# Reordering the issue of splits, control operations and a row list in the second stage of an attention and two-layer expert kernel

## The chip, the cores and the metric

One core of a Trainium2 chip. The metric is device time in microseconds (us) of the whole program. TensorE (PE) multiplies and has a queue of weight loads beside it (PEld); DVE, ACT and POOL are the vector, scalar and general engines; SP issues most of the transfers (DMA).

## The reference

Three stages follow each other on 4,608 tokens of 512 features (8 batches of 576 positions, 8 heads of 64). What is computed in the part that the change touches is the last one:

```python
attn_out = _attn_ref(q, k, v, phi)                     # attention through 32 memory slots a head
x = attn_out.transpose(0, 2, 1, 3).reshape(B * S, H * D)
x = elu(x @ w_in) @ w_out                              # 512 -> 2048 -> 512, every token
logits = x @ w_gate                                    # 8 experts
expert_idx = argmax(logits, axis=1)
gate_w = softmax(logits)[arange(N), expert_idx]
for e in range(8):
    xe = x[expert_idx == e]
    out[expert_idx == e] = gate_w[...] * (maximum(xe @ w1[e], 0) @ w2[e])   # 512 -> 1024 -> 512
```

All data is float32. Each product is made of three matmuls on pairs of rounded parts (high x high, low weights x high, high weights x low), so each operand is first "split" into a high part (a cast on ACT) and a low part (a subtraction on DVE).

## The kernel before

**First stage.** Attention and the first expert-like layer run over 16 halves of 288 tokens. At the end of each half the rows of x, times the gate, are written to a table in HBM (y_turn, y_gate, y_times on DVE, y_store on SP), and a list of the rows of each expert is scattered to another (y_scatter).

**Second stage (phase2, lines 946 to 1379).** The tokens of each expert are cut into tiles of 288. Two tiles of the expert of the first token (tiles -2 and -1, e = -2 in the code) are known early and begin while the last half is still being routed; then come 14 slots (slot(0) to slot(13), tiles 0 to 13) of full tiles, and then steps that are decided at run time (some, many). For a tile, mm1(j, f) is the first product for a block f of 128 of the 1,024 hidden features (12 matmuls of 128x128 on 288 tokens into one of two PSUM banks, ps_h), with its ReLU split into hh (ACT, L1088) and hl (DVE, L1089); mm2(j, f) adds the second product of that block (12 matmuls, ps_acc). They alternate: mm1 runs two blocks ahead of mm2, and mm1(j+1, 0) and mm1(j+1, 1) run in the last two steps (f = 6, 7) of slot j. A bank of ps_h is free again when hh and hl of the product of two before have read it.

**The weights.** load(j, i) (SP, L940) brings w1 (i = 0) or w2 (i = 1) of slot j's expert to raw[0] or raw[1], 2,048 KB each, under a condition that is read from the table ctl: where the expert is that of the slot before, it moves nothing. w1_split and w2_split (L1067 to L1074) then make the parts, 16 of them in a slot, two in each step f, for the next slot: w1 in f = 0 to 3, w2 in f = 4 to 7. In the two early tiles w2's eight splits for weights set 0 are issued between the products by hand.

**The tokens.** gather(j) (POOL, three indirect DMAs) brings the rows of a tile to the buffer xr; x_store writes them to HBM in xd and x_load reads them back to xg in another order; x_turn (DVE, four transposes) and x_split(j, c) (four chunks c: a cast on ACT, L749, and a subtraction on DVE, L750) make the operands xh and xl. Results go the other way: evac (DVE) to ot, o_store to od in HBM, o_load back to the same xr, and scatter (POOL) to the output. There is one xr, one xg, one xd and one od, so these steps of neighbouring tiles form one chain.

**The lists.** slots() computes on DVE which rows each slot has and issues an indirect DMA for the lists (its); control() computes ctl (which load to do) and the loop ends, 18 small DVE operations. columns() turns the lists by four small transposes on TensorE (L1042, L1045), with DVE operations before and behind (L1039, L1046 to L1049); gather(0) needs what it makes.

The order of the work on every engine is the order in which the program issues it (it is written out by hand under a manual schedule), and each engine takes its own instructions in that order; waits come from what an instruction reads and writes.

Of the kernel before, what the change touches and what calls it, by code (L numbers as in the profile page):

```python
# [57 lines left out]
def attn_moe_moe2_kernel(  # L58
# [112 lines left out]
    with ExitStack() as order:  # L171
        order.enter_context(tc.manual_schedule())
        setup()
        with ExitStack() as p1, ExitStack() as late_pool:
# [744 lines left out]
            mm2(b, g, f)  # L919
            y_evac(b, g)  # L920
            phase2(nc, tc, locals())


# [22 lines left out]
def phase2(nc, tc, a):  # L946
# [9 lines left out]
    early, early_w, pool, xp, x_gather, x_store, x_load, o_store, o_load, x_turn, x_split, early_gather = (  # L956
        a[n] for n in (
            "early", "early_w", "pool", "xp", "x_gather", "x_store", "x_load", "o_store", "o_load", "x_turn",
            "x_split", "early_gather",
        )  # L960
    )
# [58 lines left out]
    def control():  # L1020
        pick(sj, ind, st)
        pick(ej, ind, erow)
        V.tensor_scalar(out=later, in0=pcol, scalar1=0.0, scalar2=None, op0=ALU.is_gt)
        V.scalar_tensor_tensor(out=ctl[:, 0:1], in0=sj, scalar=pcol, in1=later, op0=ALU.is_equal, op1=ALU.mult)
        V.tensor_copy(out=ctl[:, 1:2], in_=ej)
        pick(sj, ind, ne)
        V.tensor_tensor(out=row, in0=row, in1=jm, op=ALU.add)
        V.scalar_tensor_tensor(out=row, in0=ej, scalar=-float(NR0), in1=row, op0=ALU.mult, op1=ALU.add)
        V.scalar_tensor_tensor(out=sj, in0=row, scalar=-float(T), in1=sj, op0=ALU.mult, op1=ALU.add)
        V.tensor_scalar(out=ctl[:, 2:3], in0=sj, scalar1=float(FEW), scalar2=1.0, op0=ALU.is_le, op1=ALU.add)  # L1030
        V.tensor_copy(out=ends[:, 0:1], in_=tot)
        V.tensor_copy(out=ends[:, 1:2], in_=few)
        V.scalar_tensor_tensor(
            out=ends[:, 2:3], in0=tot, scalar=float(NMIN + 1), in1=few, op0=ALU.is_gt, op1=ALU.max
        )

    def columns():
        itf = xp["r"][0:NS].rearrange("p n d -> p (n d)")[:, 0:T]
        V.tensor_copy(out=itf, in_=its)  # L1039
        ps = ps_tile(ps_m, "m")  # L1040
        for n in range(NG):
            nc.tensor.transpose(  # L1042
                ps[0:PR, NS * n:NS * n + NS], itf.rearrange("j (p n) -> j n p", n=NG)[:, n], ident[0:NS, 0:NS],
            )
        nc.tensor.transpose(ps[0:FEW, NS * NG:NS * NG + NS], itf[:, 0:FEW], ident[0:NS, 0:NS])  # L1045
        V.tensor_copy(out=idf, in_=ps[0:FEW, NS * NG:NS * NG + NS])  # L1046
        ps = ps[0:PR, 0:NG * NS]
        V.tensor_scalar(out=idx, in0=ps, scalar1=float(NT - 1), scalar2=None, op0=ALU.min)
        V.tensor_copy(out=idw, in_=ps)  # L1049

    def of(t, j):
        return lambda n: t[:, NS * n + j:NS * n + j + 1]

    def gather(j):
        for n in range(NG):
            x_gather(n, of(idx, j)(n), rows)
# [4 lines left out]
    def w1_at(p, y, c, f):  # L1061
        return wt0[:, y, 2 * c + f // HN, p, P * (f % HN):P * (f % HN) + P]

    def w1_split(p, n):
        h, l = (wt0[:, y, 2 * (n % NC) + n // NC, p] for y in range(2))
        x = raw[0][:, 512 * (2 * (n % NC) + n // NC):][:, 0:512]
        nc.scalar.copy(out=h, in_=x)  # L1067
        V.tensor_tensor(out=l, in0=x, in1=h.bitcast(F32), op=ALU.subtract)

    def w2_split(p, f, eng=V):  # L1070
        h, l = (w2t[p][:, y, f].rearrange("p (c x i) -> p c x i", c=NC, i=32) for y in range(2))
        x = raw[1][:, DM * f:DM * f + DM].rearrange("p (x c i) -> p c x i", c=NC, i=32)
        nc.scalar.copy(out=h, in_=x)
        eng.tensor_tensor(out=l, in0=x, in1=h.bitcast(F32), op=ALU.subtract)  # L1074
# [3 lines left out]
    def mm1(j, f):  # L1078
        p = max(j, 0) % 2
        xh, xl = xp[j]  # L1080
        ps = ps_tile(ps_h, "h")[:, 0:T]
        n = 0
        for y, x in ((0, xh), (1, xh), (0, xl)):
            for c in range(NC):
                nc.tensor.matmul(ps, w1_at(p, y, c, f), x[:, c], start=(n == 0), stop=(n == 3 * NC - 1))  # L1085
                n += 1
        h, l = (pool.tile([P, T], F32R, tag=f"g{x}", name=f"h{x}", bufs=3) for x in "hl")
        nc.scalar.activation(out=h, in_=ps, func=AF.Relu)  # L1088
        V.scalar_tensor_tensor(out=l, in0=ps, scalar=0.0, in1=h.bitcast(F32), op0=ALU.max, op1=ALU.subtract)  # L1089
        hq[j, f] = h, l  # L1090

    def mm2(j, f):
        p = max(j, 0) % 2
        h, l = hq.pop((j, f))
        for c in range(NC):
            if f == 0:
                acc[c] = ps_tile(ps_acc, f"acc{c}")[:, 0:T]
        for n, (y, x) in enumerate(((0, h), (1, h), (0, l))):
            for c in range(NC):
                nc.tensor.matmul(  # L1100
                    acc[c], w2t[p][:, y, f, P * c:P * c + P], x,
                    start=(f + n == 0), stop=(f == NF2 - 1 and n == 2),
                )

    def evac(j):
        ot = xp["o"]
        for c in range(NC):
            V.transpose(out=ot[:, :, c], in_=acc[c].rearrange("p (k t) -> p k t", t=32))

    def scatter(at, alone=False):  # L1110
        o_load()
        for n in range(NG):
            d = nc.gpsimd.indirect_dma_start(  # L1113
                out=out, out_offset=IndirectOffsetOnAxis(ap=at(n), axis=0), in_=xp["r"][:, n], in_offset=None,
                bounds_check=NT - 1, oob_is_err=False,
            )
            if not alone:
                rows_out(d)

    def load(j, i):  # L1120
        c, = (nc.values_load(ctl[j:j + 1, 0:1], engines=[SP], min_val=0, max_val=1),)
        ev = nc.values_load(ctl[j:j + 1, 1:2], engines=[SP], min_val=0, max_val=E - 1)
        load_raw(nc, raw[i], (w1, w2)[i], ev, c)

    def rows_out(d):
        tc.declare_no_dep(d.ins, group="rows", reason="a token's row is its own")
        tc.add_to_no_dep_group("rows", d.ins)

    def splits(j, some):
        for n in some:  # L1130
            w1_split(j % 2, n) if n < NF2 else w2_split(j % 2, n - NF2)

    def x_splits(j, some=range(NC)):
        for c in some:
            x_split(j, c)

    def slot(j):
        follow = j + 1 < NMIN
        if j > 0:
            o_store(ONE)  # L1140
        if j < NMIN - 1:
            gather(j + 2)
        if 0 < j < NMIN - 1:
            x_store()
        if j > 0:
            scatter(of(idw, j - 1))
        for f in range(NF2):
            if f + 2 < NF2:
                mm1(j, f + 2)
            elif follow:  # L1150
                mm1(j + 1, f + 2 - NF2)
            mm2(j, f)
            if f == NF2 - 1:
                evac(j)
                if not follow:
                    o_store(ONE)
                    scatter(of(idw, j))
            splits(j + 1, range(2 * f, 2 * f + 2))
            if f == 3:
                x_turn(j + 1)  # L1160
            if f in (4, 5):
                x_splits(j + 1, range(2 * f - 8, 2 * f - 6))
            if follow and f == HN - 1:
                load(j + 2, 0)
                if j == 0:
                    x_store()
            if follow and f == NF2 - 2:
                x_load()
            if follow and f == NF2 - 1:
                load(j + 2, 1)  # L1170
# [71 lines left out]
    e = -NE  # L1242
# [18 lines left out]
        y_turn(b, g, c)  # L1261
    for i in range(2):
        y_gate(b, g, i)
    y_times(b, g, 0, NB)
    y_store(b, g)
    mm1(e, 4)
    mm2(e, 2)
    w2_split(0, 4)
    w2_split(0, 5)
    control()  # L1270
    load(1, 0)
    mm1(e, 5)
    mm2(e, 3)
    for c in range(NC):
        x_split(-1, c)
    w2_split(0, 6)
    w2_split(0, 7)
    load(1, 1)
    mm1(e, 6)
    mm2(e, 4)  # L1280
    mm1(e, 7)
    mm2(e, 5)
    mm1(e + 1, 0)
    mm2(e, 6)
    mm1(e + 1, 1)
    mm2(e, 7)
    evac(e)
    mm1(e + 1, 2)
    mm2(e + 1, 0)
    columns()  # L1290
    gather(0)
    x_store()
    x_load()
    o_store(ONE)
    scatter(early_of(e))
    mm1(e + 1, 3)
# [29 lines left out]
    for j in range(NMIN - 1):  # L1326
        slot(j)
# [18 lines left out]

    first = kind(NMIN)
    slot(NMIN - 1)
    with tc.If(end > NMIN):
        either(NMIN, first)  # L1350
# [61 lines left out]
```

## Time and profile before

| | |
|---|---|
| time of three runs | 1264.07, 1264.52, 1267.41 us; median 1264.52 |
| profiled execution | 1260.01 us, its span 1258.3 us |
| busy share: PE, PEld, DVE, ACT, POOL | 96%, 88%, 63%, 53%, 36% |
| granted TensorE clock, mean | 0.985 of full speed |
| DMA | 178.41 MB, mean 142 GB/s |
| second stage | from 811.16 us (first product of tile -2) |
| slots 1 to 12 | 897.83 to 1211.06 us |

The span runs from the first to the last instruction; the time is that of the device around it. Times in the rows are counted from the span's start. The shares are averages over stages with different limits. A row of the timeline gives the start, the duration of the merged instructions, engine, line, operation with the tiles it writes and reads, the shapes and the number merged; in brackets is the idle time of the engine just before, and what ended it. "slot 2, step 6" is slot(2), f = 6.

### The profile page before, as it was taken

Reading aid. Unit: us, or ns where it says so; the run is one execution under the profiler, and the core shown is the slowest. Engines: PE = TensorE matmul, PEld = TensorE weight load, DVE = VectorE, ACT = ScalarE, POOL = GpSimd, SP = SyncE. Lnnn points to the kernel's source line nnn. Section 1 sums busy time; section 2 is a strip of 40 time slices with the busy share of each in tenths; the row PEclk is TensorE's granted clock in tenths of the full one; section 3 lists DMA queues with packets and bytes.
Section 4 is the critical chain, followed back from the end, with each engine's and each line's share of the span. In section 5 each row is a group of like instructions: output and inputs, shape, how many; then the busy total and the mean of one; then the engine's idle time right before and its main releaser. Section 6 shows DMA issues by size and latency. Waiting matters only on the chain.

```text
span 1258.3 us, 26270 instructions
## 1 busy us (share of the span) xinstructions
PE 1202.6 (96%) x10035; PEld 1110.3 (88%) x10035; DVE 789.9 (63%) x1816; ACT 664.6 (53%) x1526; POOL 450.3 (36%) x489
## 2 busy tenths in 40 slices
PE   5598899999999999999999999999999999999997
PEld 3387789899899898898899899999999999999994
DVE  6989666556556556556556535663676767767672
ACT  4687455555655555555555555522454444544542
POOL 3544244444434534434534544322212311321202
PEclk9599999999999999999999999999999999999999
DMA  9776677446356436435442271215578778566763
GB/s 260 221 220 197 175 116 153 124 96 105 106 96 105 126 75 107 136 63 112 131 64 58 69 209 33 64 21 150 153 187 255 214 215 247 151 143 191 216 212 98
DMA packets 113786, 178.41 MB, mean 142 GB/s; under 512 B 10745, under 2 KB 79609, under 8 KB 110064
## 3 DMA queue, kind: packets, MB, share of 16 engines
q1 hardware_dynamic: 105632, 157.09, 49.3%
q0 software_dynamic: 8016, 19.52, 5.5%
q8 instruction: 82, 1.34, 0.5%
q14 instruction: 56, 0.46, 0.2%
HBM read 171.62 MB, written 42.76 MB: 170 GB/s over the span
## 4 chain that ended last, share of the span: by engine, by line
PE 74%; DVE 8%; DMA 7%; issue 4%; ACT 3%; POOL 1%; SPq 1%; POOLq 0%; DVEq 0%; ACTq 0%
PE ps_acc L553 27%; PE ps_h L521 15%; PE ps_h L1085 13%; PE ps_acc L1100 11%; DMA kv<-in_v_dram 4%; PE ps_M L483 2%; PE ps_kv L381 2%; PE ps_s L425 1%; DMA out_dram<-xr,idw 1%; PE ps_l L575 1%; DVE conv_h L290 1%; DVE conv_h L293 1%; PE ps_a L373 1%; DMA xd<-xr 1%; PE ps_l L585 1%
## 5 line engine op out<-in xcount | busy, mean ns | idle before, releaser
L539 POOL TENSOR_TENSOR gl<-e,gh 128x288 fp32r<-128x288 f32 x234 | 193.4, 826 | 379.3 <-ACT gh L538 312.2
L521 PE MATMUL ps_h<-ath,wt 128*128 128x288 f32 x1024 | 260.0, 311 | 8.3 <-DVE e L531 5.6
L531 DVE SCALAR_TENSOR_TENSOR e<-e,ps_h 128x288 f32<-128x288 f32 x247 | 110.2, 447 | 205.1 <-ACT e L529 190.9
L521 PEld LDWEIGHTS ps_h<-ath,wt 128*128 128x128 f32 x1024 | 180.3, 190 | 53.1 <-issue 30.8
L538 ACT CAST gh<-e 128x288 fp32r<-128x288 f32 x247 | 106.8, 432 | 182.3 <-DVE e L531 179.2
L553 PE MATMUL ps_acc<-gh,wt 128*128 128x288 f32 x1024 | 179.2, 297 | 1.5 <-ACT gh L538 1.5
L553 PE MATMUL ps_acc<-gh,wl 128*128 128x288 f32 x1024 | 178.2, 296 | 0.0
L553 PE MATMUL ps_acc<-gl,wt 128*128 128x288 f32 x1024 | 177.4, 295 | 0.3 <-DVE gl L539 0.3
L1088 ACT ACTIVATE hh<-ps_h 128x288 fp32r<-128x288 f32 x128 | 52.7, 412 | 221.7 <-PE ps_h L1085 186.3
L1085 PE MATMUL ps_h<-xh,wt 128*128 128x288 f32 x1024 | 164.6, 300 | 1.9 <-ACT xh L749 0.7
L553 PEld LDWEIGHTS ps_acc<-gh,wt 128*128 128x128 f32 x1024 | 151.0, 190 | 3.5 <-ACT gh L538 2.4
L521 PE MATMUL ps_h<-atl,wt 128*128 128x288 f32 x512 | 151.9, 297 | 0.5 <-POOL atl L471 0.5
L1085 PEld LDWEIGHTS ps_h<-xh,wt 128*128 128x128 f32 x1024 | 144.3, 188 | 8.6 <-ACT xh L749 5.2
L553 PEld LDWEIGHTS ps_acc<-gl,wt 128*128 128x128 f32 x1024 | 150.6, 188 | 0.5 <-DVE gl L539 0.5
L553 PEld LDWEIGHTS ps_acc<-gh,wl 128*128 128x128 f32 x1024 | 150.6, 190 | 0.0
L1089 DVE SCALAR_TENSOR_TENSOR hl<-ps_h,hh 128x288 fp32r<-128x288 f32 x128 | 58.2, 455 | 120.2 <-ACT hh L1088 105.0
L528 ACT ACTIVATE e<-ps_h 128x288 f32<-128x288 f32 x256 | 104.8, 409 | 44.9 <-PE ps_h L521 43.6
L1113 POOL DMA_INDIRECT out_dram<-xr,idw x42 | 42.4, 1010 | 239.9 <-DMA xr<-od 215.1
L529 ACT ACTIVATE e<-e 128x288 f32<-128x288 f32 x256 | 113.9, 445 | 8.1
L521 PEld LDWEIGHTS ps_h<-atl,wt 128*128 128x128 f32 x512 | 98.2, 192 | 0.7 <-POOL atl L471 0.7
L1085 PE MATMUL ps_h<-xl,wt 128*128 128x288 f32 x512 | 89.5, 296 | 1.0 <-DVE xl L750 1.0
L1100 PE MATMUL ps_acc<-hh,wl 128*128 128x288 f32 x576 | 88.5, 296 | 0.0
(217 smaller groups left out, 1920.0 us busy)
## 6 DMA issues: line engine op xcount, KB each, us to landing
raw<-in_moe_w_dram SPq DMA_DIRECT2D x30, 2048.0 KB
win<-win_s SPq DMA_DIRECT2D x28, 1024.0 KB
xd<-xr SPq DMA_DIRECT2D x17, 576.0 KB
xg<-xd SPq DMA_DIRECT2D x68, 144.0 KB
kv<-in_k_dram SPq DMA_DIRECT2D x16, 576.0 KB
kv<-in_v_dram SPq DMA_DIRECT2D x16, 576.0 KB
table<-yr SPq DMA_DIRECT2D x64, 144.0 KB
od<-ot SPq DMA_DIRECT2D x64, 144.0 KB
```

The costliest lines, as they stand in the source:

```text
L521: nc.tensor.matmul(ps, x[:, u, fo:fo + P], y[:, u], start=(n == 0), stop=(n == 3 * NQ - 1))
L528: nc.scalar.activation(out=e, in_=ps, func=AF.Relu, scale=-1.0)
L529: nc.scalar.activation(out=e, in_=e, func=AF.Exp, scale=-1.0)
L531: nc.vector.scalar_tensor_tensor(out=y, in0=e, scalar=-1.0, in1=ps, op0=ALU.add, op1=ALU.max)
L538: nc.scalar.copy(out=gh, in_=e)
L539: eng.tensor_tensor(out=gl, in0=e, in1=gh.bitcast(F32), op=ALU.subtract)
L553: nc.tensor.matmul(acc[c], x[:, f, P * c:P * c + P], y, start=(first and n == 0), stop=(final and n == 2),)
L1085: nc.tensor.matmul(ps, w1_at(p, y, c, f), x[:, c], start=(n == 0), stop=(n == 3 * NC - 1))
L1088: nc.scalar.activation(out=h, in_=ps, func=AF.Relu)
L1089: V.scalar_tensor_tensor(out=l, in0=ps, scalar=0.0, in1=h.bitcast(F32), op0=ALU.max, op1=ALU.subtract)
L1100: nc.tensor.matmul(acc[c], w2t[p][:, y, f, P * c:P * c + P], x, start=(f + n == 0), stop=(f == NF2 - 1 and n == 2),)
L1113: d = nc.gpsimd.indirect_dma_start(out=out, out_offset=IndirectOffsetOnAxis(ap=at(n), axis=0), in_=xp["r"][:, n], in_offset=None, bounds_c ...
```

## The change

Issue order alone is changed. In each slot the x_splits of steps 4 and 5 are issued ahead of the splits of those steps. In the hand-written order of the two early tiles y_times and y_store move behind mm1(e, 4); the splits 5, 6 and 7 of w2 and the control operations move behind later products, splits 6 and 7 behind load(1, 1); the splits of tile -1's tokens move behind mm1(e, 6); and columns(), gather(0), x_store and x_load move from behind mm2(e+1, 0) to behind mm1(e+1, 1).

```diff
--- before.py
+++ after.py
@@ -1155,11 +1155,11 @@
                 if not follow:
                     o_store(ONE)
                     scatter(of(idw, j))
+            if f in (4, 5):
+                x_splits(j + 1, range(2 * f - 8, 2 * f - 6))
             splits(j + 1, range(2 * f, 2 * f + 2))
             if f == 3:
                 x_turn(j + 1)
-            if f in (4, 5):
-                x_splits(j + 1, range(2 * f - 8, 2 * f - 6))
             if follow and f == HN - 1:
                 load(j + 2, 0)
                 if j == 0:
@@ -1261,36 +1261,36 @@
         y_turn(b, g, c)
     for i in range(2):
         y_gate(b, g, i)
+    mm1(e, 4)
     y_times(b, g, 0, NB)
     y_store(b, g)
-    mm1(e, 4)
     mm2(e, 2)
     w2_split(0, 4)
+    mm1(e, 5)
     w2_split(0, 5)
     control()
     load(1, 0)
-    mm1(e, 5)
     mm2(e, 3)
+    mm1(e, 6)
     for c in range(NC):
         x_split(-1, c)
-    w2_split(0, 6)
-    w2_split(0, 7)
     load(1, 1)
-    mm1(e, 6)
     mm2(e, 4)
     mm1(e, 7)
+    w2_split(0, 6)
     mm2(e, 5)
     mm1(e + 1, 0)
+    w2_split(0, 7)
     mm2(e, 6)
     mm1(e + 1, 1)
+    columns()
+    gather(0)
+    x_store()
+    x_load()
     mm2(e, 7)
     evac(e)
     mm1(e + 1, 2)
     mm2(e + 1, 0)
-    columns()
-    gather(0)
-    x_store()
-    x_load()
     o_store(ONE)
     scatter(early_of(e))
     mm1(e + 1, 3)
```

## Rows read from the trace of the kernel before

**Rows 1.** Stretches: busy us of PE, PEld, DVE, ACT, POOL; clock, DMA, GB/s.
```profile
923.83:1211.06 287.23, 286.25 (x2115) 281.71 (x2114) 200.06 (x397) 141.12 (x309) 71.08 (x69) 1.00 0.72 205
840.00:847.00 7.00, 7.00 (x55) 6.79 (x54) 3.01 (x10) 0.83 (x2) 0.00 (x0) 1.00 0.00 0
```

**Rows 2.** Waits of the weight loads, slots 1 to 12: us, times, longest.
```profile
PEld ps_h L1085 <- ACT xh L749: 3.9, 12, 0.6
```

**Rows 3.** Timeline, slot 2, steps 3 to 6: start, us, engine, operation, [idle].
```profile
937.50 1.55 DVE L744 STREAM_TRANSPOSE xg<-xg 128x288 f32<-128x288 f32 x4
...
941.40 1.11 PEld L1100 LDWEIGHTS ps_acc<-hh,wl 128*128 128x128 f32 x8
...
942.09 1.13 ACT L1073 CAST w2o<-raw 128x512 fp32r<-128x512 f32 x2
...
942.74 1.29 DVE L1074 TENSOR_TENSOR w2o<-raw,w2o 128x512 fp32r<-128x512 f32 x2
...
942.99 0.32 PEld L1085 LDWEIGHTS ps_h<-xh,wt 128*128 128x128 f32 x2
...
943.12 0.77 ACT L749 CAST xh<-xg 128x288 fp32r<-128x288 f32 x2
...
943.61 1.03 PEld L1085 LDWEIGHTS ps_h<-xh,wt 128*128 128x128 f32 x6 [0.29 <-ACT xh L749]
...
945.12 1.12 PEld L1100 LDWEIGHTS ps_acc<-hh,wl 128*128 128x128 f32 x8
```

**Rows 4.** Timeline, tile -2, around y_times and the control operations.
```profile
827.73 1.36 DVE L675 TENSOR_TENSOR yr<-yr,r_g 128x1152 f32<-128x1152 f32 x1
...
829.01 0.45 DVE L1089 SCALAR_TENSOR_TENSOR hl<-ps_h,hh 128x288 fp32r<-128x288 f32 x1
...
829.51 1.10 PEld L1085 LDWEIGHTS ps_h<-xh,wt 128*128 128x128 f32 x8 [0.41 <-DVE hl L1089]
...
833.23 1.09 PEld L1085 LDWEIGHTS ps_h<-xh,wt 128*128 128x128 f32 x8 [0.49 <-DVE hl L1089]
...
833.72 2.34 SPq L940 DMA_DIRECT2D raw<-in_moe_w_dram  x2
```

**Rows 5.** Timeline, tile -1, around columns().
```profile
844.37 1.11 PEld L1100 LDWEIGHTS ps_acc<-hh,wl 128*128 128x128 f32 x8
...
845.52 0.29 DVE L1039 CAST xr<-its 23x288 f32<-23x288 int32 x1
...
846.18 0.34 PEld L1042 LDWEIGHTS ps_m<-ident,xr 23*96 23x96 f32 x3 [0.17 <-issue]
...
846.58 1.10 PEld L1085 LDWEIGHTS ps_h<-xh,wt 128*128 128x128 f32 x8
...
847.79 0.94 POOL L712 DMA_INDIRECT xr<-table,idx  x1 [14.42 <-DVE idw L1049]
```

**Rows 6.** Timeline, the first uses of the gathered tokens, tiles 0 and 1.
```profile
860.93 1.11 PEld L1100 LDWEIGHTS ps_acc<-hh,wl 128*128 128x128 f32 x8
...
861.99 1.56 DVE L744 STREAM_TRANSPOSE xg<-xg 128x288 f32<-128x288 f32 x4 [3.02 <-DMA xg<-xd]
...
865.51 1.11 PEld L1100 LDWEIGHTS ps_acc<-hh,wl 128*128 128x128 f32 x8
...
886.75 1.56 DVE L744 STREAM_TRANSPOSE xg<-xg 128x288 f32<-128x288 f32 x4 [2.72 <-DMA xg<-xd]
...
889.44 0.32 PEld L1085 LDWEIGHTS ps_h<-xh,wt 128*128 128x128 f32 x2
...
893.05 1.11 PEld L1100 LDWEIGHTS ps_acc<-hh,wl 128*128 128x128 f32 x8
```

**Rows 7.** Timeline, slot 1: a load of raw[1] and its reader.
```profile
909.80 0.00 SPq L940 DMA_DIRECT2D raw<-in_moe_w_dram  x1
...
912.79 1.13 ACT L1073 CAST wl<-raw 128x512 fp32r<-128x512 f32 x2
```

**Rows 8.** The page, DMA over the whole span.
```profile
DMA packets 113786, 178.41 MB, mean 142 GB/s; under 512 B 10745, under 2 KB 79609, under 8 KB 110064
```

## The prediction

> **What bounds the kernel now.** I read first the table of stretches, for the second stage alone. From 923.83 to 1211.06 us TensorE is busy 286.25 of 287.23 us at granted clock 1.00, while DVE has 200 us of work and ACT 141 us [rows 1]. So every product is on the path, and a change gives time only where TensorE stands still or waits. "Busy" hides part of that, since matmuls are pipelined, so I read the starts of the weight loads (PEld) as a ruler: an undisturbed product of 12 matmuls takes from its first weight load to that of the next 942.99 - 941.40 = 1.59 us [rows 3]. Every interval that is longer is time which a better order could give back. Four kinds are left.
>
> (a) One product in each slot. The product that begins at 942.99 is mm1(j+1, 0), the next slot's first; its successor begins at 945.12, so it took 2.13 us, 0.53 more than the ruler [rows 3]. After two weight loads PEld waits 0.29 us for ACT's cast of the tokens (xh, L749). The list of waits has that pair 12 times in slots 1 to 12, 3.9 us of idle time [rows 2]; the ruler costs it at 12 x 0.53 = 6.4 us, and since 3.9 is some 0.4 above 12 x 0.29, one of the 12 is longer by about 0.3. **6.7 us.**
>
> (b) The same product in slot 0. It takes 893.05 - 889.44 = 3.61 us, 2.0 above the ruler [rows 6]. DVE stood 2.72 us in x_turn(1) for the transfer xg<-xd, so all behind it in DVE's queue (hl, splits of w2, xl) came late.
>
> (c) mm1(0, 0). From 860.93 to 865.51 two products pass in 4.58 us, 1.4 above 3.19. DVE stood 3.02 us in x_turn(0), for the same kind of transfer [rows 6].
>
> (d) Two waits in tile -2: 0.41 and 0.49 us, **0.9 us** together, for hl [rows 4]. The PSUM bank of two products before is not free, because DVE does y_times (1.36 us) first, and at the second place the control operations [rows 4].
>
> **The change part by part.**
>
> *Tokens ahead of weights (lines 1158 to 1162).* No instruction is added or taken away: in steps f = 4 and 5 ACT does its two token casts before the two weight casts, and DVE its subtractions likewise. Before, ACT did the w2 casts from 942.09 (1.13 us) and the token casts of chunks 2 and 3 from 943.12 (0.77) [rows 3]. Swapped, the token casts run from 942.09 to 942.86; TensorE wants chunk 2 from 943.25 (942.99 and two weight loads). That is 0.4 to 0.8 us ahead. The low halves are wanted after eight matmuls, two thirds of a product: 942.99 + 1.06 = 944.05. DVE's two token subtractions (288 wide; the pair for w2, 512 wide, takes 1.29) can follow from 942.7. The w2 casts move to 942.86 to 944.0, before the next hh is due (mm1(j+1, 0) ends near 944.9), so nothing behind them on ACT is held, and their product is first read in the next slot. In step 4 the token casts need x_turn: its four transposes ran from 937.50 to 939.05 in chunk order, so chunk 1 is there about 938.3; ACT is through with that step's hh two products before 942.09, at 938.9. I take (a) as gone: **-6.7**. If the cover of 0.4 us fails, the old 0.53 a slot comes back.
>
> *Control later, mm1 earlier.* TensorE's own order stays as it was but for columns(); what moves is the place of DVE and ACT work between the products. hl(e, 4) now comes ahead of y_times: it can run from 827.73, where y_times began, and is done at 828.2; its user mm1(e, 6) is due at 829.1, 0.4 before it started [rows 4]. hl(e, 5) comes ahead of the control operations and of one w2 subtraction: done about 830.7 (828.2, y_times 1.36, one subtraction 0.65, which is half of 1.29, and 0.45 for itself), due 832.2, two products after 829.1. Both waits of (d) go: **-0.9**. What is made late is control, by one hl (0.45): its reader is the SP queue, whose load(1, 0) goes from 833.72 to about 834.2.
>
> *w2 splits 6 and 7 after load(1, 1).* This is a new wait. load(1, 1) writes raw[1], the buffer that these two splits read, and now stands ahead of them; so ACT's cast of split 6 waits for it, with hh of the next product, the cast of split 7 and DVE's subtraction queued behind, and TensorE waiting for mm2(e, 6). The load carries a condition. Over 840 to 847 us the DMA engines moved 0 GB/s, although both loads had been issued by 836.06 (833.72 + 2.34) [rows 1, 4]: with these inputs they move nothing. So the price is the time until a skipped load counts as done. The trace bounds it: a later one issued at 909.80 had its reader on ACT run at 912.79 without idle time before it [rows 7], so between 0 and 2.98 us. I take the middle, 1.5, as no row is nearer. Its issue: 834.2 plus the 1.7 us that the second load needs behind the first (2.34 less the wait for the subtraction of split 7, which it no longer has, about 0.6), 835.9. Cast done 835.9 + 1.5 + 0.6 (half of 1.13, rounded up) = 838.0. mm2(e, 6) is due five products after 829.1, at 837.0. Late by 1.0, about 0.15 more for the low half (a subtraction of 0.65 against four matmuls, 0.53), and a restart loss of 0.24, which (a) shows (0.53 lost for 0.29 of idle): **+1.4**, between 0 and 2.9.
>
> The Trainium skill, "DMA: Bandwidth & Descriptors", Anatomy of one DMA, gives a DMA about 2.0 us of fixed setup and completion whatever its size (it fitted them on GpSimd's path). It speaks against the change: by it this wait would be 1.9 and the sum below -7.8. No row shows what a skipped load takes, so the sum keeps the middle of the bounds.
>
> *columns() three products ahead.* Its first DVE operation (L1039) turns the list into floats, and four transposes on TensorE need it. Before, a whole product, mm2(e+1, 0) from 844.37, lay between mm1(e+1, 2) and the transposes. The copy ran at 845.52 for 0.29, behind hl of that mm1, and the transposes went at 846.18 with 0.17 of idle; the next product began at 846.58 [rows 5]. From where the product should have ended (844.37 + 1.59 = 845.96) that is 0.62. Now the transposes stand right behind mm1(e+1, 1), and the copy still stands behind that product's hl in DVE's queue. From the same rows the copy ends 845.81 - 842.78 = 3.03 us after the start of the mm1 that it follows; TensorE is at the transposes after 1.59. It stands for about 1.5 us, then 0.40 for the transposes: 1.9 instead of 0.62, **+1.3**. From below 0 (if the copy slips in while hh is awaited; the order of the queue speaks against it), from above 2.0 (one more hl in front).
>
> *What it buys.* gather(0) began at 847.79, some 1.2 us after the transposes' end at 846.58 [rows 5]. With the waits above, mm1(e+1, 1) starts near 840.0 and the transposes end near 843.5, so gather(0) goes near 844.7, 3.1 earlier. Behind it in one line stand x_store, x_load, o_store, o_load, the scatter of tile -2, gather(1), x_store, x_load, all over the one buffer xr and the SP and POOL queues; each follows the landing of the one before, so x_load(0) and x_load(1) land about 3.1 earlier. mm1(0, 0) was due at 862.5 (860.93 + 1.59) and is due at 862.5 - 0.9 + 2.7 = 864.3, so x_turn(0) is wanted 1.8 later: 4.9 in all against its wait of 3.02. Behind it TensorE is 0.4 later than before (1.8 - 1.4), so x_turn(1) has 3.5 against its 2.72 [rows 6]. Both are covered, by 1.9 and 0.8. **-1.4 and -2.0.** The evac(e) that o_store needs still runs before x_load is through.
>
> The sum: -6.7 - 0.9 - 1.4 - 2.0 = -11.0 removed, +1.4 + 1.3 = 2.7 added, **-8.3 us.** What comes behind (slot 13, the short last step, the last scatter) starts from the end of slot 13's products and moves with them. The profiled execution took 1260.01 us, 1.7 above its span; less 8.3 it would be 1251.7. The three timed runs are 4 to 7 us above it, with median 1264.52, and against that the forecast is **1256.2 us**.
>
> **The rivals.**
>
> *The transfers are not early enough.* The chain of rows 6 is long, and its cover of x_turn(1) is 0.8 us by my count. If weight loads or the od round trip hold it, (b) and (c) stay, and the prices of the earlier columns() are still paid: -6.7 - 0.9 + 2.7 = -4.9, 1259.6 us. For it: each link waits for a landing, and DVE stood there twice. Against: nothing else uses the DMA engines over 840 to 847 [rows 1].
>
> *The slots give nothing.* If the token casts then wait for x_turn in step 4, or the later w2 casts hold the next hh, (a) only changes its releaser: -8.3 + 6.7 = -1.6, 1262.9 us, within 0.3%. Against: ACT waits for TensorE before each hh in these rows, so there is slack for both.
>
> *The load is real (slower).* If load(1, 1) moved its 2,048 KB, split 6 would stand for all of it: at the 205 GB/s of rows 1 10.2 us at the 142 GB/s that is the mean of the whole profile [rows 8] 14.8. It decides from a wait of 9.7 us (11.0 - 1.3) on; at 14.8 the stall is 14.5 and the time 1264.5 + 4.8 = 1269.3 us. For it: the condition is data, and the condition of other loads is true. Against: the 0 GB/s.
>
> **How the numbers follow.** The forecast 0.70; transfers not early enough 0.15; slots give nothing 0.10; load real 0.05. A change of 0.3% (3.8 us), about what timings of this kernel tell apart, is passed by the first two: faster 0.85, same 0.10, slower 0.05. The open costs put the forecast between -11.0 + 0 + 0 = -11.0 (1253.5) and -11.0 + 2.9 + 2.0 = -6.1 (1258.4). The low end takes in that the level may be that of the profiled execution (1251.7); the high end reaches past the first rival. Range 1251 to 1261.
>
> **What would show it.** In the slots PEld must have no wait for xh of L749. In tile -2 no wait for hl before 836 us, then one for the cast L1073 of split 6 before mm2(e, 6), of 0 to 3 us, and one of about 1.5 us at the transposes of L1042. x_turn(0) and x_turn(1) must find their transfer landed. I am wrong if ACT's split 6 waits for 10 us, if x_turn still shows "DMA xg<-xd", or if the 2.13 us product stays.

## The result and the profile after

The changed kernel took 1250.71 us (median of four runs, 1248.24 to 1253.5), the kernel before 1264.48 us (four runs beside them): ratio 0.9889, 95% interval 0.9862 to 0.9917. That is faster by 13.8 us, where 8.3 had been forecast, and 0.3 us below the lower end of the range. Two longer timings of the same kernel (below) gave 0.9927 [0.9902, 0.9952] and 0.9924 [0.9902, 0.9947], 9 to 10 us; the forecast of 1256.2 against 1264.52 is a ratio of 0.9934.

The profiled execution took 1248.24 us with a span of 1246.5, 11.8 less than that of before. The second stage alone tells how much of it is the change. I count it from the first weight load of tile -2 (L1085) to the first of the short last step (L1213). First the stretch of the kernel before, then that of the kernel changed (columns as in [rows 1], the third being PEld):

```profile
811.16:1233.34 422.18, 419.27 (x3096) 411.31 (x3095) 282.96 (x609) 194.34 (x428) 96.52 (x98) 1.00 0.63 177
```

```profile
808.96:1221.66 412.70, 411.35 (x3096) 409.89 (x3095) 282.28 (x609) 194.88 (x428) 96.98 (x98) 1.00 0.65 181
```

The same instructions ran at the same clock; the stage is 9.48 us shorter. Of that, 8.1 us are idle time of the weight loads (422.18 - 411.31 = 10.9 us before, 2.8 after), and 1.4 are their own busy time (411.31 against 409.89 us for the same 3,095 loads). Another 2.2 us of the 11.8 lie ahead of the stage, which began at 808.96 instead of 811.16, and there the two programs are the same. The waits of the weight loads that are left in the second stage of the kernel changed (us, times, longest; before they had [rows 2] and the waits for hl of [rows 4]):

```profile
PEld ps_m L1042 <- issue: 1.5, 1, 1.5
PEld ps_h L1085 <- issue: 0.5, 1, 0.5
PEld ps_acc L1100 <- issue: 0.3, 1, 0.3
PEld ps_h L1085 <- DVE xl L750: 0.2, 1, 0.2
PEld ps_l L575 <- issue: 0.2, 1, 0.2
```

The twelve waits for xh are gone. The timeline of a slot of the kernel changed shows why (rows of [rows 3]):

```profile
936.61 0.76 ACT L749 CAST xh<-xg 128x288 fp32r<-128x288 f32 x2
...
937.12 0.82 DVE L750 TENSOR_TENSOR xl<-xg,xh 128x288 fp32r<-128x288 f32 x2
937.26 1.14 ACT L1073 CAST w2o<-raw 128x512 fp32r<-128x512 f32 x2
937.51 1.12 PEld L1085 LDWEIGHTS ps_h<-xh,wt 128*128 128x128 f32 x8
...
939.11 1.12 PEld L1100 LDWEIGHTS ps_acc<-hh,wl 128*128 128x128 f32 x8
```

The token cast ends at 937.37, TensorE wants chunk 2 from 937.77 (two weight loads after 937.51, as in [rows 3]): a cover of 0.40 us, as forecast. All eight high matmuls follow each other in one row, and the product takes 939.11 - 937.51 = 1.60 us instead of 2.13.

Tile -2 of the kernel changed, around y_times, and then the two loads with their reader (rows of [rows 4]):

```profile
825.54 0.46 DVE L1089 SCALAR_TENSOR_TENSOR hl<-ps_h,hh 128x288 fp32r<-128x288 f32 x1
...
825.91 1.35 DVE L675 TENSOR_TENSOR yr<-yr,r_g 128x1152 f32<-128x1152 f32 x1
...
826.85 1.12 PEld L1085 LDWEIGHTS ps_h<-xh,wt 128*128 128x128 f32 x8
...
831.88 1.74 SPq L940 DMA_DIRECT2D raw<-in_moe_w_dram  x2
...
833.63 0.62 ACT L1073 CAST wl<-raw 128x512 fp32r<-128x512 f32 x1 [1.25 <-DMA raw<-in_moe_w_dram]
834.28 0.69 DVE L1074 TENSOR_TENSOR wl<-raw,wl 128x512 fp32r<-128x512 f32 x1 [1.08 <-ACT wl L1073]
...
834.83 1.12 PEld L1100 LDWEIGHTS ps_acc<-hh,wl 128*128 128x128 f32 x8
```

hl runs ahead of y_times, and mm1(e, 6) at 826.85 finds its bank free. Below it is the new wait: ACT stands 1.25 us for load(1, 1). But the two loads are issued by 831.88 + 1.74 = 833.62, and the cast begins at 833.63: a load that is skipped counts as done within 0.01 us of its issue, so ACT waited for SP's turn and for no transfer (the DMA engines moved 0 GB/s from 833.6 to 841 us). The cast follows the issue as closely in the other six profiles that have the skipped load in this place. TensorE was held by none of it: mm2(e, 6) began at 834.83, one undisturbed product after its forerunner, with the high half there since 834.25 and the low one, which is wanted four matmuls later, at 834.97.

The neighbourhood of columns() in the kernel changed (rows of [rows 5]):

```profile
836.42 1.12 PEld L1085 LDWEIGHTS ps_h<-xh,wt 128*128 128x128 f32 x8
...
838.80 0.46 DVE L1089 SCALAR_TENSOR_TENSOR hl<-ps_h,hh 128x288 fp32r<-128x288 f32 x1 [1.99 <-ACT hh L1088]
839.17 0.29 DVE L1039 CAST xr<-its 23x288 f32<-23x288 int32 x1
839.53 0.34 PEld L1042 LDWEIGHTS ps_m<-ident,xr 23*96 23x96 f32 x3 [1.45 <-issue]
...
839.92 1.09 PEld L1100 LDWEIGHTS ps_acc<-hh,wl 128*128 128x128 f32 x8
...
841.14 0.94 POOL L712 DMA_INDIRECT xr<-table,idx  x1 [9.99 <-DVE idw L1049]
```

Here the stall came as drawn: the copy waits behind hl of mm1(e+1, 1), the transposes stand 1.45 us, and from 836.42 to 839.92 pass 3.50 us, 1.9 above the ruler of 1.59. gather(0) goes at 841.14, 32.2 us after the stage's start; before it was 847.79 - 811.16 = 36.6.

The first uses of the gathered tokens in the kernel changed, tiles 0, 1 and 2 (rows of [rows 6], and x_turn(2) with the product behind it):

```profile
857.00 1.55 DVE L744 STREAM_TRANSPOSE xg<-xg 128x288 f32<-128x288 f32 x4
...
882.26 1.56 DVE L744 STREAM_TRANSPOSE xg<-xg 128x288 f32<-128x288 f32 x4 [1.47 <-DMA xg<-xd]
...
908.47 1.56 DVE L744 STREAM_TRANSPOSE xg<-xg 128x288 f32<-128x288 f32 x4 [2.16 <-DMA xg<-xd]
...
911.69 1.12 PEld L1085 LDWEIGHTS ps_h<-xh,wt 128*128 128x128 f32 x8
...
913.46 0.19 PEld L1085 LDWEIGHTS ps_h<-xl,wt 128*128 128x128 f32 x1 [0.18 <-DVE xl L750]
913.57 1.11 PEld L1100 LDWEIGHTS ps_acc<-hh,w2o 128*128 128x128 f32 x8
```

x_turn(0) finds its tokens. x_turn(1) does not: it stands 1.47 us, with no loss for TensorE, since the token splits now run ahead of those of w2. x_turn(2), which no step of the prediction looked at, stands 2.16 us, and slot 1's product takes 913.57 - 911.69 = 1.88 us, 0.28 too long; in the two repeats it lost 1.39 and 1.23.

The tokens' chain began 4.45 us earlier, but it didn't keep that. Each time is counted from the start of the second stage:

| start of | before | changed | earlier by |
|---|---|---|---|
| gather(0) | 36.63 | 32.18 | 4.45 |
| x_load for tile 0 | 45.97 | 41.58 | 4.39 |
| o_load | 52.53 | 49.33 | 3.20 |
| gather(1) | 61.20 | 58.11 | 3.09 |
| x_store for tile 1 | 67.04 | 64.70 | 2.34 |
| x_turn(1) | 75.59 | 73.30 | 2.29 |
| x_load for tile 2 | 95.22 | 93.19 | 2.03 |
| x_turn(2) | 100.77 | 99.51 | 1.26 |

The first loss, 1.19, lies almost whole between o_store (43.50 instead of 47.83, still 4.33 earlier) and o_load. SP's wait for that landing from 840 to 890 us (us, times, longest), in the kernel before:

```profile
SPq L738 <- DMA od<-ot: 4.1, 4, 1.7
```

and in the kernel changed:

```profile
SPq L738 <- DMA od<-ot: 5.5, 4, 3.0
```

The longest wait for that landing is 1.3 us longer. The next loss, 0.75, is the landing of gather(1), for which x_store waits, and the last, 0.77, that of x_load for tile 2. Why the same transfers land later in the new order no row shows. It stays open.

### The profile page after: what moved, and what is told of

It is laid out like the page before. It is cut to its first block, busy times and chain, and to the rows that moved or that the text cites. A ratio compares the mean times of both kernels' runs of the same rounds, so it can differ in the third digit from the quotient of the medians.

```text
span 1246.5 us, 26270 instructions
## 1 busy us (share of the span) xinstructions
PE 1192.0 (96%) x10035; PEld 1107.1 (89%) x10035; DVE 788.6 (63%) x1816; ACT 664.5 (53%) x1526; POOL 450.0 (36%) x489
## 4 chain that ended last, share of the span: by engine, by line
PE 82%; DMA 6%; DVE 6%; issue 3%; ACT 1%; POOL 1%; SPq 1%; POOLq 0%; DVEq 0%; ACTq 0%
PE ps_acc L553 29%; PE ps_h L521 16%; PE ps_h L1085 15%; PE ps_acc L1100 15%; DMA kv<-in_v_dram 3%; PE ps_M L483 2%; PE ps_kv L381 2%; DMA out_dram<-xr,idw 1%; PE ps_s L425 1%; DMA win_x<-in_moe_w_in_dram 1%; PE ps_l L575 1%; DVE conv_h L290 1%; PE ps_a L373 1%; PE ps_l L585 1%; DVE conv_h L293 1%
## 5 line engine op out<-in xcount | busy, mean ns | idle before, releaser
L1085 PE MATMUL ps_h<-xh,wt 128*128 128x288 f32 x1024 | 157.4, 296 | 0.0
L1085 PEld LDWEIGHTS ps_h<-xh,wt 128*128 128x128 f32 x1024 | 143.1, 188 | 0.5 <-issue 0.5
L1085 PE MATMUL ps_h<-xl,wt 128*128 128x288 f32 x512 | 89.2, 296 | 0.0
```

## The experiments

Two theories stood after the result. **A:** the change acts in the second stage alone, by some 9 us, and the rest of the 13.8 is the spread of the stage ahead of it. **B:** something of the change acts outside the second stage too, or sizes are off by more than the trace shows.

To compare runs I put, for each profiled execution but that of e6_real, the time that products lost against the ruler (worked out from the starts of the weight loads: an interval of 12 loads less 1.595 us), by place, beside the length of the second stage. "columns" is the product ahead of the transposes and the transposes themselves; "slots 2 to 12" is the sum.

| kernel | tile -2 | columns | mm1(0,0) | slot 0 | slot 1 | slots 2 to 12 | stage |
|---|---|---|---|---|---|---|---|
| before | 1.0 | 0.6 | 1.4 | 2.0 | 0.5 | 6.1 | 422.18 |
| e2_null (before) | 1.0 | 0.6 | 1.4 | 2.6 | 1.6 | 6.1 | 424.07 |
| changed | 0 | 1.9 | 0 | 0 | 0.3 | 0 | 412.70 |
| e1_again (changed) | 0 | 1.9 | 0 | 0 | 1.4 | 0 | 413.94 |
| e10_again2 (changed) | 0 | 1.9 | 0 | 0 | 1.2 | 0 | 413.28 |
| e3_slots | 1.0 | 0.6 | 1.5 | 1.5 | 2.4 | 0 | 417.12 |
| e4_early | 0 | 1.9 | 0 | 1.5 | 2.1 | 5.9 | 421.59 |
| e5_oldcols | 0 | 0.6 | 1.4 | 0.9 | 2.3 | 0 | 417.17 |
| e7_loadlate | 0 | 1.9 | 0 | 0 | 2.4 | 0 | 414.64 |
| e8_best | 0 | 0.6 | 0 | 0.6 | 0 | 0 | 412.90 |
| e9_cols2 | 0 | 0.6 | 0 | 0 | 0 | 0 | 410.75 |

Lone products that lost 0.1 to 1.3 us elsewhere in some runs (0.37 at 1025.18 in the kernel changed) stand in the length of the stage, not in the columns. Each row is one profiled execution; the stages of the two of the kernel before differ by 1.9 us.

**The same kernels again.** e1_again and, in another run, e10_again2 are the kernel changed without an edit; e2_null is the kernel before without an edit.

> The changed kernel once more, timed in more rounds. Theory A (the change acts in the second stage alone; its products lie 9.5 us closer together, and what the first timing showed beyond that is spread of the first stage): second stage from its first product to the first product of the short last step 412.7 us again (422.2 before), and a gain over before that comes nearer to 9.5 us, between 8 and 12. Theory B (something in the change also shortens the first stage, by 2 to 4 us): the gain stays at 12 to 14 us, and the second stage starts 2 us or more earlier than in the kernel before in every profile.

> The kernel changed once more, unaltered. If the change acts in the second stage alone and the rest of the first timing was the spread of the first stage, it is 8 to 12 us faster than the kernel before (ratio 0.990 to 0.994) and the second stage takes 412.5 to 414 us. If something of it acts outside that stage, it is 13 us or more faster.

> The kernel before as a candidate against itself, to see what two identical programs differ by. Theory A: the times differ by less than 0.3%, single executions by up to 4 us, and the start of the second stage in the profile moves by about 2 us around 811 us without any change. Theory B: the second stage starts at 811 us within 0.5, and times agree as closely.

Measured: e1_again 0.9927 [0.9902, 0.9952], 1256.56 against 1266.58 us; e10_again2 0.9924 [0.9902, 0.9947], 1258.50 against 1267.47; e2_null 1.0001 [0.9973, 1.0029]. The stages are 413.94 and 413.28 against 424.07 us. So the change is worth 9 to 10 us, and about as much is missing from the second stage: the mean of the three changed, 413.31, is 9.8 below the mean of the two of before, 423.13. Nor did the stage begin earlier in the repeats: at 813.88 and 818.27 us, against 811.16 and 812.44 in the two profiles of before. Behind the stage every profiled execution took 24.8 to 25.3 us. B falls.

Where the rest of the first timing can come from shows in the stage ahead, which is the same in all kernels: the second stage began between 808.96 us (the kernel changed, first timing) and 822.23 us (e6_real). One place shows how. In e4_early TensorE stood 3.36 us at L381, where in the kernel changed that wait was 1.7. The row of the weight load names no releaser, that of its matmuls names the transfer of v. First the two rows of e4_early, then its stretches (columns as in [rows 1]), then the same stretches of the kernel changed:

```profile
304.39 2.35 PEld L381 LDWEIGHTS ps_kv<-kv,a 96*32 96x32 f32 x48 [3.36 <-issue]
304.43 2.78 PE L381 MATMUL ps_kv<-kv,a 96*32 96x128 f32 x48 [3.15 <-DMA kv<-in_v_dram]
```

```profile
304.00:308.00 4.00, 3.57 (x51) 3.22 (x52) 0.00 (x0) 0.38 (x1) 0.00 (x0) 0.56 0.57 43
308.00:312.00 4.00, 4.00 (x20) 4.00 (x20) 1.78 (x8) 1.29 (x3) 0.81 (x1) 0.59 0.89 235
```

```profile
304.00:308.00 4.00, 4.00 (x32) 4.00 (x31) 3.67 (x13) 2.12 (x6) 1.33 (x2) 1.00 0.75 210
308.00:312.00 4.00, 4.00 (x33) 4.00 (x32) 3.87 (x6) 1.71 (x6) 2.54 (x3) 1.00 1.05 227
```

Behind the longer wait the granted clock was 0.56 and 0.59, mostly the lower of its two levels (1.2 GHz), and from 308 to 312 us TensorE did 20 matmuls instead of 33. So 1.7 us more of a wait drew behind it some 1.6 us (4 less 20/33 of 4) of slow matmuls in these 4 us alone. All the waits of the weight loads at L381 ahead of the second stage sum to 6.0 us in the kernel changed, 7.7 in the kernel before, 9.7 in e4_early and 11.5 in e6_real. That this spread alone made 13.8 out of 9 or 10 is what the repeats support, and it isn't shown for those four runs.

**Slots alone.** The order of token and weight splits is changed in the kernel before, and nothing else:

```diff
+            if f in (4, 5):
+                x_splits(j + 1, range(2 * f - 8, 2 * f - 6))
             splits(j + 1, range(2 * f, 2 * f + 2))
             if f == 3:
                 x_turn(j + 1)
-            if f in (4, 5):
-                x_splits(j + 1, range(2 * f - 8, 2 * f - 6))
```

> Only the slots' part: tokens split ahead of weights in steps 4 and 5, the two early tiles as before. Theory A: the twelve products of 2.13 us shrink to 1.59 (6.7 us), and slot 0's long product loses some 0.8 of its 2.0 us since the low halves come earlier behind the late x_turn(1): 7.5 us less in all, the waits of tile -2 and at mm1(0, 0) unchanged. Rival (the slots' gain depends on the earlier token chain): less than 5 us.

Measured: 0.9943 [0.9914, 0.9972], stage 417.12, 6.0 below the mean of before where 7.5 had been expected. The eleven slots from slot 2 on lose nothing. Slots 0 and 1 still lose 1.5 and 2.4 us, slot 1 more than before (0.5 and 1.6): their x_turn waits for its transfer. From 840 to 930 us DVE stood in x_turn (us, times, longest):

```profile
DVE xg L744 <- DMA xg<-xd: 10.8, 3, 4.3
```

**The early tiles alone.** The same diff the other way round, in the kernel changed, so that the hand-written order is new and the slots are old.

> Only the early tiles' part: the hand-written order of the change, the slots in their old order. Theory A: tile -2's waits (0.9), mm1(0, 0)'s (1.4) and slot 0's (2.0 less the 0.53 that every slot keeps) go, the transposes cost 1.3, and slot 1, whose x_turn(2) now waits for its transfer, pays more than the 0.53: 2 to 3 us less in all. Rival (the early order is worth nothing by itself, what it saves comes back at the transposes and in slot 1): within 1 us of before.

Measured: 0.9965 [0.9938, 0.9993], stage 421.59. This is 1.5 below the mean of before, between what was expected (2 to 3) and the rival (within 1), and less than the two profiles of before differ by; what the edit does is read from the places. The eleven slots lose 0.53 to 0.55 each again. In the waits of the weight loads from 815 to 1199 us both sides of the new order show, the old wait and the new stall:

```profile
PEld ps_h L1085 <- ACT xh L749: 3.9, 14, 0.3
PEld ps_h L1085 <- DVE xl L750: 2.3, 4, 1.3
PEld ps_m L1042 <- issue: 1.5, 1, 1.5
```

By their stages, against the mean of before, the parts are worth 6.0 (slots) and 1.5 us (early tiles), 7.5 in all, and together 9.8. They seem to help each other in slots 0 and 1: the early gather makes x_turn's wait shorter, and the slots' new order lets a wait of 1.5 us pass without a loss. Alone each leaves 3.6 to 3.9 us there, together 0.3 to 1.4. (The ratios, 0.57% and 0.35%, don't resolve this.)

**columns() back.** The kernel changed, with the list turned in its old place:

```diff
     mm1(e + 1, 1)
-    columns()
-    gather(0)
-    x_store()
-    x_load()
     mm2(e, 7)
...
     mm2(e + 1, 0)
+    columns()
+    gather(0)
+    x_store()
+    x_load()
```

> The changed kernel with columns(), gather(0), x_store and x_load back in their old place behind mm2(e+1, 0). Theory A (the earlier list costs 1.3 us at the transposes and pays for the waits on transfers in x_turn): the stall of 1.5 us at the transposes goes; back come mm1(0, 0)'s 1.4, some 1.5 in slot 0 and 2 in slot 1; the second stage is 3 us longer than with the change (about 416 against 412.7 to 414.0). Rival (the early list is worth no more than it costs): the same length within 0.7 us.

Measured: 0.9896 [0.9856, 0.9937] over four runs, too wide to tell it from the kernel changed; stage 417.17, 3.9 above the mean of the kernel changed, 1.8 of it in two lone products at 1185 us. The stall at the transposes is gone (1.9 falls to 0.6), and mm1(0, 0) and slots 0 and 1 lose 4.6 us where the kernel changed loses 0.3 to 1.4. Moving columns() costs 1.3 and buys more than 3.

**A load that is real.** load(1, 1) of the kernel changed without its condition, so that it brings 2,048 KB that are already there:

```diff
-        load_raw(nc, raw[i], (w1, w2)[i], ev, c)
+        load_raw(nc, raw[i], (w1, w2)[i], ev, None if (j, i) == (1, 1) else c)
```

> The changed kernel with load(1, 1) made unconditional: it now moves 2,048 KB of w2, the same rows that raw[1] holds, since slot 1 has slot 0's expert. Theory A (a skipped load counts as done when it is issued, so the new wait costs nothing, and a real one would cost its whole transfer): ACT waits 8 to 15 us for it before the cast of split 6, TensorE 7 to 14 us before mm2(e, 6), and most of the gain of the change is gone or more. Rival (the wait is never on the path): TensorE waits under 1 us.

Measured: 0.9988 [0.9957, 1.0019], stage 423.65, 10.3 above the mean of the kernel changed: the whole gain is spent. The issue of the two loads, the reader of the second and the product behind it, then the stretches:

```profile
845.07 1.94 SPq L940 DMA_DIRECT2D raw<-in_moe_w_dram  x2
...
855.08 0.62 ACT L1073 CAST wl<-raw 128x512 fp32r<-128x512 f32 x1 [9.42 <-DMA raw<-in_moe_w_dram]
...
855.75 1.94 PEld L1100 LDWEIGHTS ps_acc<-hh,wl 128*128 128x128 f32 x8 [7.58 <-ACT wl L1073]
```

```profile
850.00:856.00 6.00, 0.25 (x1) 0.26 (x2) 0.27 (x1) 0.92 (x3) 0.00 (x0) 0.53 0.73 268
856.00:863.00 7.00, 5.76 (x29) 5.52 (x29) 2.04 (x5) 0.92 (x3) 0.00 (x0) 0.67 0.00 0
```

With the load as good as alone the DMA engines moved 268 GB/s, so the wait was 9.4 us, and from the end of the issue (845.07 + 1.94 = 847.01) to the cast 8.1 passed, where the rival had 14.8 by the mean of 142 [rows 8]. TensorE lost 7.6 us in the wait, and behind it the granted clock was 0.67 for some 7 us: eight weight loads took 1.94 instead of 1.12 us, and the next two products lost 1.2 and some 0.9. So the condition is what the new place of split 6 rests on: with a real load there the change is worth nothing.

**The load later.** The kernel changed, with load(1, 1) behind w2_split(0, 7), which takes the new wait away:

```diff
         x_split(-1, c)
-    load(1, 1)
     mm2(e, 4)
...
     w2_split(0, 7)
+    load(1, 1)
```

> The changed kernel with load(1, 1) issued behind w2's splits 6 and 7 again. Theory A (the skipped load is free): ACT's wait of 1.25 us before the cast of split 6 goes, and the second stage keeps its length of 412.7 to 414.0 us within the 1.1 us that slot 1's x_turn(2) varies by. The step of the prediction (the wait costs 1.4 us): 1.4 us shorter.

Measured: 0.9886 [0.9829, 0.9943], from two runs only; stage 414.64, not shorter than the kernel changed. ACT's wait for raw is gone and no product of the early tiles starts sooner: the wait cost nothing. What it lost is in slot 1 (2.4 us), where x_turn(2) stood 4.3 us. That is the longest of the kernels with the new order, and the repeats of the kernel changed have 3.3 and 3.1; whether the later load makes the difference is open.

**The copy ahead, and the store of tile -1 later.** The first part of columns(), the copy on DVE, becomes a function of its own (floats) and is issued ahead of mm1(e+1, 1); o_store and the scatter of tile -1 go behind x_store in slot 0:

```diff
     mm2(e, 6)
+    floats()
     mm1(e + 1, 1)
     columns()
...
                 if j == 0:
                     x_store()
+                    o_store(ONE)
+                    scatter(early_of(-1))
...
     evac(-1)
-    o_store(ONE)
-    scatter(early_of(-1))
```

> Two more edits on the changed kernel: DVE's copy ahead of the transposes is issued one product earlier, and the scatter of tile -1 moves into slot 0, behind x_store of tile 2, so that gather(2) need not wait for it. Theory A: the 1.5 us before the transposes shrink to under 0.3, x_turn(2) no longer waits (2.2 to 3.3 us before) and slot 1's long product (0.3 to 1.4 us) goes: 1.8 to 2.9 us shorter than the change. Rival (the stall is that of the transposes' own operands or of the landing of the lists): the wait before L1042 stays at 1 us or more.

Measured: 0.9878 [0.9837, 0.9919], stage 412.90, not shorter than the changed kernel's 412.70, so the expected gain of 1.8 to 2.9 us did not come. The transposes wait 0.17 us instead of 1.45, a gain of 1.3, and x_turn(2) has no wait; but gather(0) goes only 0.9 earlier (31.3 us after the stage's start), x_turn(1) now stands 2.5 us and slot 0's product loses 0.6; three lone products behind slot 1 lost 1.6 more.

**columns() one product earlier still.** e8_best, with the copy behind mm1(e+1, 0) and columns() and what hangs on it ahead of mm1(e+1, 1):

```diff
     mm1(e + 1, 0)
+    floats()
     w2_split(0, 7)
     mm2(e, 6)
-    floats()
-    mm1(e + 1, 1)
     columns()
     gather(0)
     x_store()
     x_load()
+    mm1(e + 1, 1)
```

> The changed kernel with the copy for the transposes issued right behind mm1(e+1,0), and the transposes, gather(0), the store and the load of the tokens ahead of mm1(e+1,1), behind mm2(e,6). If the tokens' chain starts late because gather(0) is late, the wait at the transposes stays under 0.3 us, gather(0) is issued some 1.5 us earlier after the first product of tile -2 than in the kernel changed, the waits for x_turn(1) and x_turn(2) shrink to under 1 us, and the second stage, 412.7 to 413.9 us in the kernel changed, takes 410.5 to 411.5. If the chain is bound by its own transfers and not by its start, the waits for x_turn(1) and x_turn(2) stay at 1.5 us or more and the stage takes 412.5 us or more.

Measured: 0.9883 [0.9854, 0.9912], 1253.96 us, where e10_again2 on the same chip had 0.9924 and 1258.50. The stage takes 410.75 us, inside the 410.5 to 411.5 of the first theory and 2.5 below e10_again2. gather(0) goes 29.3 us after the stage's start, 2.0 earlier than in e8_best. x_turn(1) is down to this (waits of DVE, 805 to 960 us), and x_turn(2) has no wait:

```profile
DVE xg L744 <- DMA xg<-xd: 0.2, 1, 0.2
```

No product of the 14 slots lasts over 1.66 us. So the chain was bound by its start. It is the fastest of the kernels by its stage; by the timings its interval and that of the kernel changed still touch.

## Why the prediction was right or wrong

The mechanism was right in the main. Two steps failed: the price of the wait on load(1, 1), which took 0.01 us and not 1.5, and the level from which the sum was counted, the median of three timings, which spreads by more than the sum's error.

**(a) Slots, -6.7: right.** The product takes 1.60 us with the forecast cover of 0.40. e3_slots and e4_early show that this edit alone decides it: 0 and 5.9 us lost in slots 2 to 12, against 6.1 before.

**(b), (c) Slot 0 and mm1(0, 0), -2.0 and -1.4: right in size, half right in cause.** Both losses are gone, and e5_oldcols brings the second back whole and half of the first. x_turn(0) found its transfer landed. For x_turn(1) the cover of 0.8 us wasn't there: DVE waited 1.47 us for "DMA xg<-xd", which the prediction had named as a sign of being wrong. Two things make up the difference of 2.3. DVE arrived 1.0 us earlier than before instead of 0.4 later, since the 1.4 of load(1, 1) were not paid. And the step that said that both loads land some 3.1 earlier took the chain's lead as constant, where it fell from 4.45 us at gather(0) to 2.29 at x_turn(1). The wait of 1.47 cost nothing because of (a)'s new order. With it, waits of x_turn(1) up to 1.8 us cost slot 0 nothing (e7_loadlate) and one of 2.5 cost 0.6 (e8_best); with the old one a wait of 2.2 cost 1.5 (e4_early) and one of 2.7 cost 2.0 (the kernel before).

**(d) Tile -2, -0.9: right.** Both waits for hl are gone (1.0 by the ruler). No run undoes this edit alone; the waits stay away in e5_oldcols and e7_loadlate, each of which takes back another edit of the early tiles.

**The new wait on load(1, 1), +1.4: wrong.** The term took 1.5 us, the middle of 0 to 2.98, for a skipped load to count as done. It took 0.01 us or less, in seven profiles. All else of the step held: the loads were issued by 24.7 us after the stage's start, and mm2(e, 6) came at 25.9 (reckoned: 24.7 and 25.8). The wait of 1.25 us on ACT cost TensorE nothing, and e7_loadlate, without it, was no faster. This is the mis-sized term of the sum; with 0 in its place the sum is -9.7.

The Trainium skill, "DMA: Bandwidth & Descriptors", Anatomy of one DMA, would have put 2.0 us in place of the 1.5. It says that most of the fixed time is the receipt of the last byte in the target memory. The trace, with 0.01 us and 0 GB/s behind the issue, doesn't agree: the figure is not to be used for a load that is skipped.

**Transposes, +1.3: right**, 1.9 instead of 0.6, in e1_again, e4_early, e7_loadlate and e10_again2 too.

**What was left out.** "What is late next" was asked for x_turn(0) and x_turn(1), not for x_turn(2). There DVE arrives 3.1 us earlier than before and the transfer 1.3, so slot 1 loses 0.3 to 1.4 us. With the terms as measured, -6.7 - 1.0 - 1.4 - 2.0 + 1.3 + 0.3 = -9.5, which is the -9.48 of the two profiled stages.

**The level: wrong.** The sum was made for the profiled execution and carried to the median. For the first timing that gave 1256.2 against 1250.71, 5.5 us too high, and the sum makes only 1.2 of that (-8.3 against -9.48). With both open costs at nothing the prediction had 1253.5, so the load's price alone doesn't explain a time below the range. The other 4.3 lie outside the second stage if its gain was that of the two profiles: 2.2 show there as its earlier start, and the rest is not shown for these runs. In the longer timings the gain is 9 to 10 us, and 1256.56 and 1258.50 stand beside medians of before that are 2 to 3 us above that used; that they come near the forecast of 1256.2 is in part luck. The stage ahead spreads by some 13 us over the profiled executions, and four timings don't average that out.

**The rivals.** "Not early enough" was true in part (x_turn(1), x_turn(2)), and cost 0.3 to 1.4 us, not the 3.4 of (b) and (c). "Slots give nothing" fell. "The load is real" was the right mechanism for another input: e6_real lost 10.3 us, less than the 13.1 (14.5 less 1.4) of the rival by its DMA rate.

## What to carry to other kernels

Where matmuls follow each other without idle time in the busy shares, take the starts of the weight loads as a ruler: each interval above that of an undisturbed product is time that an order can give back, and here these intervals, 11.6 us before and 2.2 after, make up all but 0.1 of the 9.48 by which the stage became shorter. When the wait at one link of a chain of transfers is taken away, follow the chain to where it is late next, with the lead of each link read anew, as a lead is not carried on whole. And before a load that a condition skips is priced, look at whether it is skipped: here it is 0 or 10 us.

## What the runs showed of the hardware

A transfer that its condition skips counts as done at once: ACT's cast ran 0.01 us or less after the issue of the second load ended, in all seven profiles that have it, while from the first issue to the end of the second 1.74 us passed on SP's queue (the kernel changed). The same load, made real, had its reader run 8.1 us after the issue, at 268 GB/s (e6_real). A single idle stretch of TensorE of 3.36 us (e4_early) or 7.6 us (e6_real) was followed by 7 to 8 us at a granted clock of 0.56 to 0.67, where a wait of 1.7 us (the kernel changed, first stage) and of 1.45 us (its transposes) was followed by 1.00.
